# Block-causal attention and a gated convolution unit on one core: reciprocals spread by eight small transfers and a shuffle, attention output two pairs at a time, the first nine pairs interleaved anew

## Chip, cores and metric

The kernel runs on one core of a Trainium2 chip. The metric is the device time of the execution in microseconds (us). Before the change it is 261.77 us, the median of 13 runs (260.62 to 264.54).

## What is computed

Eight batches, eight heads, 576 positions of 64 features: attention in which a block of 64 positions sees itself and the blocks before it, and behind it a gated unit over the 512 joined features, with a causal convolution of five taps as the gate. Cut to what matters:

```python
scores = scale * np.matmul(q, k.transpose(0, 1, 3, 2))
scores = np.where(block_i >= block_j, scores, -1e9)
attn = np.exp(scores - np.max(scores, axis=-1, keepdims=True))
attn = attn / (np.sum(attn, axis=-1, keepdims=True) + 1e-09)
x = np.matmul(attn, v)                        # heads side by side: [8, 576, 512]
gate_pre = sum(conv_w[k] * xp[:, k:k + S, :] for k in range(5))
gate = 1.0 / (1.0 + np.exp(-gate_pre))
out = (gate * (x @ w_val)) @ w_out
```

All inputs and the output are fp32.

## The kernel before

The unit of work is a pair of heads of one batch: 32 pairs, t = 4b + n for pair n of batch b. The main loop (L398) takes one pair an iteration and runs on for LAG = 10 more, since the later stages of a pair follow in later iterations.

**Inputs.** `load_pair(hb)` loads q and k of half a batch (two pairs) as fp32 tiles `st` by four transfers on SyncE's queue (L99) and casts each to fp16 on GpSimd (L103), with VectorE and ScalarE in its place for the first half batch. Four buffers of `st` are there, so a load waits for the cast of two half batches before. The call for half batch t/2 + 3 stands in iteration t. `load_v` and `cast_v` (L106 to L124) do the same for v, once a batch, with one fp32 buffer and eight casts on GpSimd; the weights go through `st` too (L373 to L381). Matmuls and SyncE's transfers keep the order of the program (L43 to L47); on the other engines a scheduler chooses the order. Each transfer signals one of eight semaphores in turn, and waits until the transfer before it on the same semaphore has landed.

**Scores.** `trans` (L129) transposes a half batch in three parts of six 128 x 128 blocks on TensorE, and VectorE copies them out of PSUM into `qkT` (L143). `scores` (L157) makes a pair's scores transposed (keys on partitions) in four PSUM tiles, of which two buffers exist (`psS`), and ScalarE turns each into `pt` by an exp (L172, L197). No maximum is subtracted.

**Denominators.** `den` (L217) sums the columns of `pt` for the four pairs of a batch by matmuls with one-hot weights `oh`: row 32 * (2h + half) + n of the tile `dn` holds pair n's sums of head h and half block. VectorE takes the reciprocal `ri` (L250) of all 128 rows. `spread` (L253) brings them to the partitions that need them: `ri` to a DRAM scratch `r_scratch` (L255), and from there four broadcasts, each of four rows to 64 partitions, into `rb` (L260): 1.18 MB a batch.

**Attention output.** `pv` (L267) multiplies `pt` with v into two PSUM tiles `x` a pair, and VectorE multiplies them with `rb` into `xb` (L307), in fp16, features on partitions.

**Gated unit.** `gate` (L318) is the convolution as five matmuls with diagonal weights `diag` a half, and a tanh on ScalarE (L329); `val` (L332) multiplies `xb` of all four pairs by w_val, and VectorE joins both into `gv` (L346); `project` (L350) multiplies by w_out, 36 tiles in all, each copied on ScalarE (L357) and stored by its queue (L358). `conv_weights` (L361) makes `convT` and the 20 blocks of `diag` on VectorE (L369), in iterations 5 to 8.

All PSUM tiles but the scores' (`tr`, `dn`, `x`, `cv`, `vp`, `ot`) share one pool of four buffers, `psG` (L76).

The order within iteration t, by which TensorE's work is queued: scores of t (all of them at once while t < 10, later the first two tiles only), one output tile, `den` of the batch before where t is a multiple of 4, the loads, `spread` one iteration after `den`, `pv` of pair t - 6, the other two score tiles, `gate` of pair t - 10, a part of the transposes, `val` of pair t - 10, another part, another output tile.

Of the kernel before, what the change touches and what calls it, by code (L numbers as in the profile page):

```python
# [10 lines left out]
def kernel(  # L11
# [20 lines left out]
    nc = tc.nc  # L32
# [5 lines left out]

    B, H, S, D = q.shape
    NT = B * 4  # L40
    rscr = nc.dram_tensor("r_scratch", [B, 128, 288], fp32, kind="Internal")

    def mm(**kw):  # L43
        tc.keep_in_program_order(nc.tensor.matmul(**kw))  # L44

    def load(**kw):
# [11 lines left out]
    conv_nat = cpool.tile([5, 512], fp32, tag="conv_nat")  # L58
    convT = cpool.tile([128, 4, 5], fp32, tag="convT")
    diag = cpool.tile([128, 4, 5, 128], fp16, tag="diag")  # L60
    NXB = 3
    xbs = [cpool.tile([128, 4, S + 4], fp16, tag=f"xb{i}", name=f"xb{i}")
           for i in range(NXB)]
    vzs = [cpool.tile([128, 4, 6, 64], fp16, tag=f"vz{i}", name=f"vz{i}") for i in range(2)]

    stg = ctx.enter_context(tc.tile_pool(name="stg", bufs=4))
# [9 lines left out]
    psG = ctx.enter_context(tc.tile_pool(name="psG", bufs=4, space=PSUM))  # L76

    make_identity(nc, ident)
    nc.vector.tensor_copy(out=ident16[:, :], in_=ident[:, :])  # L79
    nc.vector.memset(oh[:, :, :], 0.0)  # L80
    for o, rows in enumerate((slice(0, 128), slice(0, 64), slice(64, 128))):
        nc.vector.memset(oh[rows, o, :].rearrange("p (m r) -> p m r", r=4)[:, :, 3:4], 1.0)
    for xb in xbs:
        nc.vector.memset(xb[:, :, 0:4], 0.0)
    for vz in vzs:
        nc.gpsimd.memset(vz[64:128, :, 0:5, :], 0.0)
        nc.gpsimd.memset(vz[0:64, :, 5, :], 0.0)
# [41 lines left out]
    def trans(hb, part):  # L129

        b, half = divmod(hb, 2)
        if b not in qkT:
            qkT[b] = qkp.tile([128, 4, 2, S], fp16, tag="qkT", name="qkT")
        tr = psG.tile([128, 6, 128], fp16, tag="G")
        slots = [divmod(6 * part + s, 9) for s in range(6)]
        for s, (w, c) in enumerate(slots):
            tc.keep_in_program_order(nc.tensor.transpose(  # L137
                out=tr[:, s, :], in_=q16[hb, w][:, c, :, :], identity=ident16[:, :]))
        for w in range(2):
            ss = [s for s in range(6) if slots[s][0] == w]  # L140
            if ss:
                c0 = slots[ss[0]][1]
                nc.vector.tensor_copy(  # L143
                    out=qkT[b][:, 2 * half:2 * half + 2, w, :].rearrange(
                        "p n (x c) -> p n x c", c=9)[:, :, :, c0:c0 + len(ss)],
                    in_=tr[:, ss[0]:ss[-1] + 1, :].rearrange("p c (x n) -> p n x c", n=2))
# [10 lines left out]
    def scores(t, part):  # L157
# [8 lines left out]
        def full(ps, h, i, lo):  # L166
            f = 64 * first_q(h, i)
            mm(out=ps[:, h, lo:lo + S - f], lhsT=kT[h][:, f - 64:f + 64], rhs=qT[h][:, f:S],
               start=True, stop=True, skip_group_check=True)
# [5 lines left out]
        if part == 0:  # L175
# [9 lines left out]
            full(ps, 1, 2, 320)  # L185
            ex(1024, ps[:, :, :], 1024)
            return
        ps = psS.tile([128, 2, 512], fp32, tag="S")
        full(ps, 0, 2, 0)
        q4 = [x.rearrange("d (j x) -> d j x", x=64) for x in qT]  # L190
        mm(out=ps[64:128, 1, 0:256], lhsT=kT[1][:, 0:64], rhs=q4[1][:, 1:8:2, :],
           start=True, stop=True, skip_group_check=True)
        for i in range(4):
            f = 64 * (2 * i + 1)
            mm(out=ps[0:64, 1, 64 * i:64 * i + 64], lhsT=kT[1][:, f:f + 64],
               rhs=qT[1][:, f:f + 64], start=True, stop=True, skip_group_check=True)
        nc.scalar.activation(  # L197
            out=pt[:, 2048:2560].rearrange("p (h x) -> p h x", h=2),
            in_=ps[:, :, 0:256], func=AF.Exp, bias=0.0, scale=0.125)
        ps = psS.tile([128, 2, 512], fp32, tag="S")  # L200
        mm(out=ps[64:128, 0, 0:320], lhsT=kT[1][:, 0:64], rhs=q4[1][:, 0:9:2, :],
           start=True, stop=True, skip_group_check=True)
# [9 lines left out]


    ris = {}
    rbs = {}

    def den(b):  # L217

# [33 lines left out]

    def spread(b):  # L253

        load(out=rscr[b], in_=ris.pop(b)[:, :])  # L255
        rb = rp.tile([128, 4, 2, 288], fp32, tag="rb")
        for h in range(2):
            for e in range(2):
                r0 = 32 * (2 * h + e)
                load(  # L260
                    out=rb[64 * h:64 * h + 64, :, e, :],
                    in_=rscr[b, r0:r0 + 4, :].rearrange("(a r) x -> a r x", a=1).to_broadcast(
                        [64, 4, 288]))
        rbs[b] = rb


    def pv(t):  # L267
        b, n = divmod(t, 4)
        pt = pts.pop(t)
        v16, vd, vz = vts[b]  # L270
        xb = xbs[b % NXB]
        for part, (lo, hi) in enumerate(((0, 5), (5, 9))):
            nb = hi - lo
            x = psG.tile([128, nb, 64], fp32, tag="G")
# [27 lines left out]
            for z in range(max(len(x_) for x_ in todo)):  # L302
# [4 lines left out]
            nc.vector.tensor_tensor(  # L307
                out=xb[:, n, 4 + 64 * lo:4 + 64 * hi].rearrange("p (j e y) -> p j e y", e=2, y=32),
                in0=x[:, :, :].rearrange("p j (e y) -> p j e y", e=2),
                in1=rbs[b][:, n, :, :].rearrange("p e (j y) -> p j e y", y=32)[:, lo:hi],  # L310
                op=ALU.mult)


# [45 lines left out]
                          in_=ob[:, :])  # L359

    def conv_weights(g):  # L361
        if g == 0:
            ps = psG.tile([128, 4, 16], fp32, tag="G")
            for i in range(4):
                mm(out=ps[:, i, 0:5], lhsT=conv_nat[0:5, 128 * i:128 * i + 128],
                   rhs=ident[0:5, 0:5], start=True, stop=True, skip_group_check=True)
            nc.vector.tensor_copy(out=convT[:, :, :], in_=ps[:, :, 0:5])
        for j in range(5):
            nc.vector.tensor_scalar(out=diag[:, g, j, :], in0=ident16[:, :],  # L369
                                    scalar1=convT[:, g, j:j + 1], scalar2=0.0,  # L370
                                    op0=ALU.mult, op1=ALU.add)
# [22 lines left out]
    load_pair(2)  # L394

    proj = []
    LAG = 10
    for t in range(NT + LAG):  # L398
        b, r = divmod(t, 4)
        m = t - LAG  # L400
        hb = (t + 3) // 2 if t % 2 else t // 2 + 1
        tr = [(hb, part) for part in ((1, 2), (0,))[t % 2]] if hb < 2 * B else []
        if t < NT:
            scores(t, 0)
            if m < 0:
                scores(t, 1)
        if t == 0:
            trans(1, 0)
        if proj:
            project(*proj.pop(0))  # L410
        if r == 0 and 1 <= b <= B:
            den(b - 1)
        if t % 2 == 0:
            load_pair(t // 2 + 3)
        if r == 0 and b < B:
            load_v(b)
        if t in (2, 3, 6, 7):
            weights(t // 4, t % 2 * 2)
        if r == (2 if b else 1) and b < B:
            cast_v(b)  # L420
        if r == 1 and 1 <= b <= B:
            spread(b - 1)
        if 0 <= t - 6 < NT:
            pv(t - 6)
        if 0 <= m and t < NT:
            scores(t, 1)
        if 5 <= t < 9:
            conv_weights(t - 5)
        if 0 <= m < NT:
            gate(*divmod(m, 4))  # L430
        if tr:
            trans(*tr.pop(0))
        if 0 <= m < NT:
            val(*divmod(m, 4))
            u, i = divmod(m, 8)
            if i == 3:
                proj.extend((u, j) for j in range(4))
            if i == 7:
                proj.extend((u, j) for j in range(4, 9))
        if tr:  # L440
            trans(*tr.pop(0))
        if proj:
            project(*proj.pop(0))
# [32 lines left out]
```

## Time and profile before

The times are those of one profiled execution on the slowest core (here the only one).

| | |
|---|---|
| profiled execution | 261.69 us |
| its span, first to last instruction | 259.9 us |
| TensorE matmul (PE) | 222.1 us busy, 85% |
| TensorE weight load (PEld) | 154.1 us, 59% |
| VectorE (DVE) | 124.7 us, 48% |
| ScalarE (ACT) | 136.4 us, 52% |
| GpSimd (POOL) | 91.5 us, 35% |
| moved by DMA | 50.94 MB, 196 GB/s |
| chain that ended last: `rb<-r_scratch` and `r_scratch<-ri` | 8% and 7% of the span |

A row of the profile names the source line, the engine, the operation, the output and the input, then the busy time and mean time of one. "issue" stands for time in which an engine waited for nothing that the profile shows; SPq is the queue of SyncE, which only issues transfers. A busy TensorE need not be at its peak: ends of matmuls are modelled. The shares are averages over stages that differ much, so that the tables by stage are to be read first.

### The profile page before, as it was taken

What the parts mean: (1) busy time and instruction counts of PE and PEld (TensorE: products, weight loads), DVE (VectorE), ACT (ScalarE), POOL (GpSimd) and SP (SyncE); (2) the same over time, 40 slices, a digit from 0 to 9 for tenths busy, and PEclk for the clock granted to TensorE, in tenths of its full rate; (3) what the DMA queues carried; (4) which work ended last, traced back from release to release, by engine and by line L of the source; (5) the groups of instructions that cost most, each with busy time, mean ns of one, the idle gap of its engine ahead of it and who ended that gap; (6) DMA issues with size and microseconds to landing.
All of it is one profiled execution on the core that took longest, in us unless ns stands there. A gap on an engine that the chain in (4) does not pass through costs nothing.

```text
span 259.9 us, 7172 instructions
## 1 busy us (share of the span) xinstructions
PE 222.1 (85%) x3064; PEld 154.1 (59%) x3064; DVE 124.7 (48%) x230; ACT 136.4 (52%) x230; POOL 91.5 (35%) x108
## 2 busy tenths in 40 slices
PE   0387787658788898988999999999999999999993
PEld 0255375437556665666667766776676667667661
DVE  2532447954544653474446545663456326254130
ACT  0357637412744465655665666556655661332533
POOL 5444952826283382315730564063005300000000
PEclk9999996757799999999999999999999999999999
DMA  6999586898789959887995699666816421921305
GB/s 193 310 291 261 200 237 152 170 344 249 157 177 366 211 116 304 296 203 156 339 282 157 160 322 281 179 149 156 226 55 159 117 83 34 238 98 43 139 27 202
DMA packets 34730, 50.94 MB, mean 196 GB/s; under 512 B 2437, under 2 KB 20869, under 8 KB 34698
## 3 DMA queue, kind: packets, MB, share of 16 engines
q1 hardware_dynamic: 29504, 41.03, 59.7%
q10 hardware_dynamic: 5194, 9.45, 9.7%
q8 instruction: 24, 0.39, 0.7%
q14 instruction: 8, 0.07, 0.1%
HBM read 39.86 MB, written 10.62 MB: 194 GB/s over the span
## 4 chain that ended last, share of the span: by engine, by line
PE 62%; DMA 18%; ACT 9%; DVE 6%; SPq 3%; issue 2%; DVEq 0%; ACTq 0%
PE cv L44 14%; PE ot L44 11%; PE vp L44 10%; PE ps L44 9%; DMA rb<-r_scratch 8%; ACT pt L172 8%; DMA r_scratch<-ri 7%; PE x L44 6%; PE dn L44 6%; PE tr L137 6%; SPq L47 3%; DVE qkT L143 3%; DVE ri L250 2%; DMA st<-in_k_dram 2%; DMA out_dram<-ob 1%
## 5 line engine op out<-in xcount | busy, mean ns | idle before, releaser
L172 ACT ACTIVATE pt<-ps 128x1024 f16<-128x1024 f32 (+1 forms) x96 | 76.1, 828 | 47.8 <-PE ps L44 47.5
L143 DVE COPY qkT<-tr 128x768 f16<-128x768 f16 (+1 forms) x64 | 50.1, 830 | 45.1 <-PE tr L137 45.0
L44 PE MATMUL ps<-qkT 64*64 64x64 f16 (+10 forms) x608 | 49.7, 269 | 14.4 <-ACT pt L172 12.5
L103 POOL CAST t<-st 128x1152 f16<-128x1152 f32 x30 | 34.3, 1145 | 44.6 <-DMA st<-in_q_dram 24.8
L44 PEld LDWEIGHTS <-qkT 64*64 64x64 f16 (+1 forms) x608 | 24.3, 110 | 38.3 <-issue 30.3
L44 PE MATMUL cv<-xb,diag 128*128 128x288 f16 x320 | 45.5, 286 | 1.6 <-DVE xb L307 1.1
L357 ACT COPY ob<-ot 128x512 f32<-128x512 f32 x36 | 21.3, 591 | 36.4 <-PE ot L44 34.9
L346 DVE SCALAR_TENSOR_TENSOR gv<-th,vp 128x288 f16<-128x288 f32 x64 | 27.2, 447 | 27.5 <-PE vp L44 27.0
L307 DVE TENSOR_TENSOR xb<-x,rb 128x320 f16<-128x320 f32 x64 | 26.2, 445 | 29.3 <-PE x L44 19.9
L116 POOL CAST t<-st 128x2304 f16<-128x2304 f32 x8 | 16.9, 2106 | 65.6 <-PE x L44 53.3
L137 PE MATMUL tr<-ident,t 128*128 128x128 f16 x288 | 28.2, 250 | 13.7 <-DVE ident L79 6.9
L44 PE MATMUL vp<-xb,w_val_sb 128*128 128x288 f16 x256 | 37.0, 286 | 2.0 <-issue 1.3
L329 ACT ACTIVATE th<-cv 128x288 f32<-128x288 f32 x64 | 26.2, 410 | 23.0 <-PE cv L44 22.8
L44 PE MATMUL ot<-w_out_sb,gv 128*128 128x512 f16 x144 | 35.8, 380 | 0.3
L44 PEld LDWEIGHTS <-diag 128*128 128x128 f16 x320 | 28.9, 97 | 11.7 <-issue 2.0
L137 PEld LDWEIGHTS <-t 128*128 128x128 f16 x288 | 22.8, 112 | 16.5 <-DVE t L103 6.8
L44 PE MATMUL x<-pt,t 128*64 128x256 f16 (+3 forms) x384 | 28.4, 261 | 1.6 <-DVE qkT L143 1.5
L44 PEld LDWEIGHTS <-w_val_sb 128*128 128x128 f16 x256 | 24.1, 98 | 8.3 <-issue 2.0
L44 PEld LDWEIGHTS <-t 128*64 128x64 f16 x384 | 18.9, 114 | 10.1 <-issue 7.6
L250 DVE RECIPROCAL ri<-dn 128x288 f32<-128x288 f32 x8 | 15.7, 1957 | 19.2 <-PE dn L44 19.2
L197 ACT ACTIVATE pt<-ps 128x512 f16<-128x512 f32 x32 | 19.2, 599 | 5.5 <-PE ps L44 5.5
L44 PEld LDWEIGHTS <-gv 128*128 128x128 f16 x144 | 12.9, 98 | 15.0 <-issue 2.3
(31 smaller groups left out, 138.2 us busy)
## 6 DMA issues: line engine op xcount, KB each, us to landing
st<-in_q_dram SPq DMA_DIRECT2D x32, 288.0 KB, 6.3
st<-in_k_dram SPq DMA_DIRECT2D x32, 288.0 KB, 6.0
rb<-r_scratch SPq DMA_DIRECT2D x32, 288.0 KB, 5.5
out_dram<-ob ACTq DMA_DIRECT2D x36, 256.0 KB, 2.7
r_scratch<-ri SPq DMA_DIRECT2D x8, 144.0 KB, 2.6
st<-in_moe_w_val_dram SPq DMA_DIRECT2D x2, 512.0 KB, 7.2
st<-in_moe_w_out_dram SPq DMA_DIRECT2D x2, 512.0 KB, 8.1
st<-in_v_dram SPq DMA_DIRECT2D x8, 0.2 KB, 9.8
```

Of the source, the lines that this page charges most:

```text
L44: tc.keep_in_program_order(nc.tensor.matmul(**kw))
L103: cast(out=t[:, :, :, :], in_=st[:, :, :, :].rearrange("p z c d -> p c z d"))
L116: nc.gpsimd.tensor_copy(out=t[:, :, :], in_=st[:, :, :])
L137: tc.keep_in_program_order(nc.tensor.transpose(out=tr[:, s, :], in_=q16[hb, w][:, c, :, :], identity=ident16[:, :]))
L143: nc.vector.tensor_copy(out=qkT[b][:, 2 * half:2 * half + 2, w, :].rearrange("p n (x c) -> p n x c", c=9)[:, :, :, c0:c0 + len(ss)], in_=t ...
L172: nc.scalar.activation(out=pt[:, o:o + w], in_=src, func=AF.Exp, bias=0.0, scale=0.125)
L197: nc.scalar.activation(out=pt[:, 2048:2560].rearrange("p (h x) -> p h x", h=2), in_=ps[:, :, 0:256], func=AF.Exp, bias=0.0, scale=0.125)
L250: nc.vector.reciprocal(out=ri[:, :], in_=dn[:, :, :].rearrange("p j x -> p (j x)"))
L307: nc.vector.tensor_tensor(out=xb[:, n, 4 + 64 * lo:4 + 64 * hi].rearrange("p (j e y) -> p j e y", e=2, y=32), in0=x[:, :, :].rearrange("p ...
L329: nc.scalar.activation(out=th[:, HF * hf:HF * hf + HF], in_=cv[:, :], func=AF.Tanh, bias=0.0, scale=0.5)
L346: nc.vector.scalar_tensor_tensor(out=gvs[u][:, g, c0:c0 + HF], in0=th[:, HF * hf:HF * hf + HF], scalar=1.0, in1=vp[:, :], op0=ALU.add, op1 ...
L357: nc.scalar.copy(out=ob[:, :], in_=ot[:, :])
```

## The change

Five things change together.

- `spread` no longer goes through DRAM. Eight transfers of 4 rows x 288 values (4.6 KB) take `ri` from SBUF to a tile `rq` (two of them, filled with 1.0 at the start) so that in each quadrant of 32 partitions the rows 0 to 3 hold the four pairs' reciprocals of both half blocks of that head. For batch 0 the four transfers of the first head go by ScalarE's queue.
- `pv` begins with a shuffle on VectorE, which copies row n of each quadrant of `rq` to all its 32 rows, 576 fp32 elements, into a `rb` for this pair alone.
- `pv` runs for two pairs in the iterations t = 4b + 3 (pairs 0 and 1 of batch b - 1) and t = 4b + 4 (pairs 2 and 3), and in the other two not at all; the third and fourth score tile stand between the two. LAG is 9.
- While t < 9, `scores` goes in three parts (two tiles, one, one), with parts of the transposes between them. `conv_weights` moves to iterations 0 to 4.
- At the start ScalarE runs a dummy exp of one column, and copies the second part of the first half batch's transposes in VectorE's place.

In the changed program VectorE meets the first shuffle of a batch two iterations after the reciprocal for batches 0 and 1 and at the end of the reciprocal's own iteration from batch 2 on. For batch 0 ScalarE's four issues stand within and behind the exps of iteration 5.

The diff, cut to its core:

```diff
-    rscr = nc.dram_tensor("r_scratch", [B, 128, 288], fp32, kind="Internal")
...
+    rqs = [cpool.tile([128, 2, 288], fp32, tag=f"rq{i}", name=f"rq{i}") for i in range(2)]
...
+    nc.vector.memset(coefs[:, :], 0.0)
+    nc.scalar.activation(out=coefs[:, :], in_=coefs[:, :], func=AF.Exp, bias=0.0, scale=1.0)
...
+    for rq in rqs:
+        nc.gpsimd.memset(rq[:, :, :], 1.0)
...
-                nc.vector.tensor_copy(
+                evac = nc.scalar.copy if hb == 0 and part == 1 else nc.vector.tensor_copy
+                evac(
...
-        load(out=rscr[b], in_=ris.pop(b)[:, :])
-        rb = rp.tile([128, 4, 2, 288], fp32, tag="rb")
+        ri = ris.pop(b)
         for h in range(2):
-            for e in range(2):
-                r0 = 32 * (2 * h + e)
-                load(
-                    out=rb[64 * h:64 * h + 64, :, e, :],
-                    in_=rscr[b, r0:r0 + 4, :].rearrange("(a r) x -> a r x", a=1).to_broadcast(
-                        [64, 4, 288]))
-        rbs[b] = rb
+            for u in range(2):
+                for e in range(2):
+                    r0, r1 = 32 * (2 * h + u), 32 * (2 * h + e)
+                    move = nc.scalar.dma_start if b == 0 and h == 0 else load
+                    move(out=rqs[b % 2][r0:r0 + 4, e, :], in_=ri[r1:r1 + 4, :])
...
+        rb = rp.tile([128, 2, 9, 32], fp32, tag="rb")
+        nc.vector.stream_shuffle(out=rb[:, :, :, :].rearrange("p e j y -> p (e j y)"),
+                                 in_=rqs[b % 2][:, :, :].rearrange("p e x -> p (e x)"),
+                                 mask=[n] * 32)
...
-                in1=rbs[b][:, n, :, :].rearrange("p e (j y) -> p j e y", y=32)[:, lo:hi],
+                in1=rb[:, :, lo:hi, :].rearrange("p e j y -> p j e y"),
...
-    LAG = 10
+    LAG = 9
...
+        if t == 0:
+            tr.insert(0, (1, 0))
         if t < NT:
             scores(t, 0)
-            if m < 0:
-                scores(t, 1)
-        if t == 0:
-            trans(1, 0)
-        if proj:
-            project(*proj.pop(0))
-        if r == 0 and 1 <= b <= B:
-            den(b - 1)
...
+        if t <= 4:
+            conv_weights(t - 1)
+        if proj:
+            project(*proj.pop(0))
+        if r == 0 and 1 <= b <= B:
+            den(b - 1)
+        if m < 0 and tr:
+            trans(*tr.pop(0))
+        for n in range(2):
+            if r == 3 and 1 <= b <= B:
+                pv(4 * b - 4 + n)
+            if r == 0 and 2 <= b <= B + 1:
+                pv(4 * b - 6 + n)
+            if n == 0 and t < NT:
+                if 0 <= m:
+                    scores(t, 1)
+                    scores(t, 2)
+                else:
+                    scores(t, 1)
+                    if tr:
+                        trans(*tr.pop(0))
+        if m < 0 and t < NT:
+            scores(t, 2)
         if r == 1 and 1 <= b <= B:
             spread(b - 1)
-        if 0 <= t - 6 < NT:
-            pv(t - 6)
-        if 0 <= m and t < NT:
-            scores(t, 1)
-        if 5 <= t < 9:
-            conv_weights(t - 5)
```

## The prediction

> **What bounds the kernel now.** I read the windows by stage first, the chain second, then the time lines of the queues. Let t be the loop's pair number; the four denominators of t = 4, 8, 12, 16 begin at 33.3, 59.6, 83.4 and 110.9 us in TensorE's time line, which gives the stretches below (microseconds, busy time of PE, PEld, DVE, ACT, POOL with instruction counts, granted clock, DMA share, GB/s).
>
> ```profile
> 13.07:32.90 19.83, 15.35 (x133) 9.35 (x133) 6.97 (x9) 13.58 (x19) 12.17 (x14) 1.00 0.84 245
> 32.90:59.60 26.70, 19.05 (x260) 14.28 (x259) 17.17 (x34) 11.79 (x17) 13.28 (x16) 0.72 0.84 225
> 59.60:82.90 23.30, 18.87 (x314) 14.13 (x313) 11.90 (x20) 10.59 (x18) 11.54 (x14) 0.88 0.87 233
> ...
> 138.20:163.50 25.30, 24.74 (x382) 17.23 (x382) 13.36 (x24) 16.68 (x29) 10.75 (x12) 1.00 0.80 226
> ```
>
> A full stage (138 to 163) is TensorE work from end to end. The first three do a third to two thirds of such a stage's work in as much time. Why, the chain tells (start, length, what):
>
> ```profile
> 38.21 6.96 DMA r_scratch<-ri
> ...
> 47.18 7.97 DMA rb<-r_scratch
> ...
> 55.23 0.50 DVE xb L307
> ...
> 64.27 6.80 DMA r_scratch<-ri
> ...
> 73.06 6.52 DMA rb<-r_scratch
> ...
> 79.66 0.50 DVE xb L307
> ```
>
> From 38 to 55 and from 64 to 80 us nothing but the reciprocals' way to DRAM and back ends the waits. Behind it SP's queue stands still, so the next loads leave late; and they are late already, as SyncE's and GpSimd's time lines show:
>
> ```profile
> 24.44 2.11 POOL L116 CAST t<-st 128x2304 f16<-128x2304 f32 x1 [3.74 <-DMA st<-in_v_dram]
> 30.80 2.23 POOL L103 CAST t<-st 128x1152 f16<-128x1152 f32 x2
> ...
> 31.97 1.20 SPq L47 DMA_DIRECT2D st<-in_q_dram  x2
> 33.27 1.19 SPq L47 DMA_DIRECT2D st<-in_k_dram  x2
> 34.92 0.71 SPq L47 DMA_DIRECT2D st<-in_v_dram  x1
> 38.21 4.22 SPq L47 DMA_DIRECT2D r_scratch<-ri  x1
> 45.19 2.61 SPq L47 DMA_DIRECT2D rb<-r_scratch  x4
> 47.89 2.11 SPq L47 DMA_DIRECT2D st<-in_q_dram  x2
> ```
>
> The values of batch 0 land at 24.4, GpSimd casts them until 30.7, and only then the fifth half batch of q and k (needed at t = 5), whose staging buffers the sixth waits for. The load of v sent at 34.9 lands at 44.9, and r_scratch, queued behind it, at 45.2.
>
> **TensorE's work at the full clock**, start to start in the time line around 104 to 112 us: scores 1.12 a pair, six transposes 0.34 (16 half batches x 3), attention output 0.84, conv 1.24, value product 0.98, one output tile 0.97, denominators 1.54 a batch. From t = 10 on (68.8 us) there remain 22 scores 24.6, 29 transposes 9.9, 6 denominators 9.2, 28 outputs 23.5, 32 conv 39.7, 32 value 31.4, 36 tiles 34.9: 173.2. With 4.0 from the last matmul to the end, the 191.1 us to 259.9 hold 13.9 of loss. So the kernel's time is the start of t = 10, plus 173.2, plus 4.0, plus losses, and the change is to be costed in these terms.
>
> **Head.** The table load (1.28 us at 7.88, right before k's cast) moves ahead, behind the wait for k: gain 1.3. Two of the four PSUM copies go from DVE to ACT, which then runs two of about 0.5 (estimate from ACT's 436 ns for 320 and 599 for 512 elements) beside DVE's 0.96: together scores start at about 11.3, not 13.1. The GpSimd fills of rq (two of 576 elements; 1.16 us was measured for 1280) lie in its idle 5.1 us before the first cast: nothing.
>
> **t = 0 to 4.** Now scores, exps and transposes take turns: ACT has 2.98 a pair (1.94 + 0.60 + 0.44) and pairs start at 18.2, 22.0, 26.4, 30.2: about 4.1 apart. With transposes put between score parts the pitch falls to the larger of ACT's 2.98 and TensorE's. Here a row and a rule differ: the clock row says full speed until 40 us, but the same seven score matmuls take 1.03 there and 0.61 at 90 us. TensorE: Matmul & The Clock Gate (Part 1, The HAM clock gate) says that the array starts at half clock until it has been busy for a window of some 3.4 us, and warns that the recorded clock is not to be trusted alone. By the row TensorE needs 1.12 + 0.51 = 1.6 a pair; by the durations 2.0 + 1.05 = 3.05. I take 3.2, and the den of t = 4 in between: t = 5 starts at 30. The 20 diag instructions (7.8 us of DVE), moved from t = 5..8 to t = 1..4, make DVE 17.9 us busy from 11.3 on, until 29.2: just covered; in the kernel now they hold a transposed tile back by 1.3 us at 52.
>
> **t = 5 to 9.** The loads rule: the casts for t = 5, 6 end at about 31.4 and 32.5 as now (0.5 earlier), those for t = 7, 8 at 36.7 and 40.6. The spread leaves 8 transfers of 4.6 KB instead of 147 KB out and four broadcasts of 288 KB back (9.4 MB of the 50.9 in all). For batch 0 four go out on ACT's queue: 4 x 0.56 of issue there, and the last waits until w_val has landed (34), at worst 1.4 us of exps behind it. The other four stand in SP's queue behind v of batch 1, as r_scratch does now, and land with it at 45.3. The next q, k loads leave at 40.6 instead of 47.9. Two pairs of attention output at t = 7 take all four PSUM buffers; they come free when VectorE has shuffled (two of 0.75) and multiplied: 47.2. den of t = 8 waits for that, about 5 us. Then VectorE's order is counted through: reciprocal until 52.0, copies 53.3, products 54.2, copy 55.1, products 56.0; TensorE starts t = 9 at 54.3, conv and value product included now, and t = 10 at **58.1** instead of 68.8.
>
> **The shuffle** has no row. Below: the slope of the product (474 ns for 320, 416 for 256 elements: 0.91 ns an element) gives 0.71 for 576; above: the reciprocal's 1.96 for 288 elements would give 3.7. VectorE: DVE Perf Modes (the perf-mode tier table) has it at one element a cycle, some 2400 ns for 2048, which with the same fixed part is 0.77. I take 0.75, near the product's row since both read one element at a time: 32 x 0.75 = 24 us, VectorE 124.7 to 149 of 250. A stage has 13.4 to 15.2 us of VectorE in 25 to 28; 3 more stay under it. From 3.7 us a shuffle it would be the bound.
>
> **A rule against the change.** DMA: Bandwidth & Descriptors (Rules for kernel authors) says to coalesce small transfers; under 64 KB one pays mostly overhead (its Anatomy of one DMA puts the fixed part at some 2 us). Eight in a row, waited for one by one, would be 16 us. The rows: a DMA issue takes SP 0.61 us, r_scratch lands after 1.8 to 2.6 from 110 us on, 5.7 to 7.0 before. So 8 x 0.61 + 1.8 = 6.7 after the reciprocal, against 1.8 + 2.6 + 5.5 = 9.9 now. I take 6.7 for late batches, 10 to 12 for the first.
>
> **Full stages.** SP's other loads stand behind 4.9 us of issues instead of about 4.4 of waiting and issuing: even. From batch 2 on, VectorE's first shuffle waits at the end of t = 4b + 4 for the spread, with copies and gate products queued behind it. Counted through, VectorE reaches it 5.3 us after the reciprocal, and TensorE can go on for 4.9 more before it lacks a buffer; less the 2.4 of shuffles and copy behind it, a landing up to 7.8 us after the reciprocal costs nothing. What does cost: in two of four iterations no attention output lies between scores any more. TensorE has 0.55 + 0.97 + 0.28 us before the third score tile, whose buffer the second exp frees at 2.45: 0.65 lost, twice a batch: 1.3 x 5 batches = 6.5. Given back: the two waits for rb at 79 and 101 us (1.1 + 1.0) and the half-clock stretch at t = 10 (1.2 to 1.4). Losses 13.9 - 2.1 - 1.4 + 6.5 = 16.9. Conv and value product of one pair (2.2) are done by t = 10, so 171.0 remain.
>
> **Sum:** 58.1 + 171.0 + 4.0 + 16.9 = 250.0 of span; the profiled run has 1.8 outside its span (261.69 and 259.9) and lies 0.1 under the median: about 251.5.
>
> **Rivals.** (1) As summed, own range 246 to 257: half the chance. (2) The early waits are shorter: SP's half of the first spread isn't held by v's load, so that products come at 41 and t = 10 at 53, and the third tile's wait is partly covered (losses 12): 53 + 171 + 4 + 12 + 1.8 = 242. For it: four transfers on ACT's own queue; against: r_scratch landed 0.3 us after v. 0.25. (3) The early gain is mostly hidden: TensorE falls back to half clock in the 5 us wait, den, outputs and copies each late, t = 10 at 64: 258. The clock row's 0.50 at 55 to 60 us speaks for it. 0.12. (4) Slower: the shuffle at the head of VectorE's queue. If the eight transfers land as r_scratch does early (7.0) in every batch, 4.9 + 7.0 = 11.9 is 4.1 over the 7.8, in 6 batches: 25 us, 276. It decides from 9.5 us after the reciprocal (1.7 a batch eats the gain of 10.3). Against it: 1.8 us landings from 140 us on. 0.13.
>
> **Numbers.** 251.5; range 241 to 261, which takes in (2) and (3) and leaves out (4) and a little under (2). Within 0.2%, what a measurement can hardly tell from no change, 0.03; faster 0.84; slower 0.13.
>
> **What would show it.** Score start near 11.3; pairs 3.2 apart until t = 4; first product near 47; t = 10 near 58; DMA about 42 MB; shuffles of 0.75; per full stage two waits of TensorE for exp of 0.65; products never waiting for a spread after 110 us. Wrong if shuffles take over 1.5, if spreads land more than 9 us after a reciprocal in full stages, or if t = 10 starts after 66.

## The result, and the profile after

The changed kernel takes 256.45 us, the median of 11 runs (254.24 to 258.59); the kernel before, run beside it, 262.37 us (48 runs). The ratio is 0.9775, with a 95% interval of 0.9747 to 0.9803: 2.2% faster. The prediction was 251.5 us in a range of 241 to 261. The profiled execution of the changed kernel took 258.59 us (span 256.8), the slowest of its eleven and 2.1 us above the median, so that its early stages have to be held against other runs, as is done below.

First the windows by stage, as before: TensorE's time line has the denominators of t = 4, 8, 12 at 28.6, 47.0 and 75.5 us (33.3, 59.6 and 83.4 before). The columns are the stretch, its length, the busy time of PE, PEld, DVE, ACT and POOL with counts, granted clock, DMA share, GB/s.

```profile
11.90:28.59 16.69, 15.56 (x134) 9.72 (x135) 13.75 (x30) 11.83 (x17) 9.63 (x11) 0.84 0.90 258
28.59:47.00 18.41, 14.07 (x249) 10.10 (x248) 10.25 (x16) 13.04 (x18) 9.82 (x10) 0.87 0.72 204
47.00:75.52 28.52, 24.70 (x347) 18.18 (x347) 17.84 (x37) 11.96 (x21) 19.62 (x24) 0.82 0.75 218
131.43:158.72 27.29, 25.47 (x384) 17.73 (x382) 17.10 (x34) 16.29 (x29) 10.75 (x12) 1.00 0.55 172
```

From the first scores to the denominators of t = 4, and from there to those of t = 8, it takes 16.7 and 18.4 us instead of 20.2 and 26.3. In the third row, 347 matmuls need 24.70 us of TensorE at a granted clock of 0.82. The last row is a full stage: 27.29 us long where the like one before had 25.30, with TensorE busy 25.47 of it instead of 24.74 of 25.30. So the start won and the full stages lost.

The chain (start, length, what) at the place where before r_scratch and rb had stood:

```profile
35.22 7.76 DMA rq<-ri
...
43.00 1.74 DMA rq<-ri
...
45.06 0.86 DVE rb L278 x2
...
46.45 0.50 DVE xb L316
...
47.00 2.90 PE dn L43 x72
```

One way of the reciprocals in place of two: it ends at 44.7 instead of 55.2. SyncE's and GpSimd's time lines for the same stretch:

```profile
24.09 2.11 POOL L121 CAST t<-st 128x2304 f16<-128x2304 f32 x1 [4.09 <-DMA st<-in_v_dram]
30.48 2.23 POOL L108 CAST t<-st 128x1152 f16<-128x1152 f32 x2
...
34.79 0.71 SPq L46 DMA_DIRECT2D st<-in_v_dram  x1
37.35 6.23 SPq L46 DMA_DIRECT2D rq<-ri  x4
43.68 1.27 SPq L46 DMA_DIRECT2D st<-in_q_dram  x2
```

The values still land at 24.1 and hold GpSimd until 30.5. Four small transfers behind v's next load keep SyncE's queue for 6.23 us (3.16 of them the first issue alone, the one directly behind that load), and the loads of q and k leave at 43.7 (47.9 before). The shuffle's row of the page (busy time, mean ns of one), and that of the loads' queue (packets, MB, share):

```profile
L278 DVE STREAM_SHUFFLE rb<-rq 128x576 f32<-128x576 f32 x32 | 24.8, 806 | 0.1
...
q1 hardware_dynamic: 20128, 30.69, 41.0%
```

In the page before, that queue had moved 41.03 MB, and the whole 50.94 instead of 40.62.

The account in stages, by the starts of the denominators in the time line: t = 12 comes 7.9 us earlier (75.5 for 83.4). From t = 12 to t = 32 the five stages take **137.2 us instead of 130.1**:

```profile
83.38:213.46 130.08, 124.22 (x1880) 85.64 (x1877) 66.97 (x120) 81.79 (x142) 47.46 (x55) 1.00 0.74 201
75.52:212.68 137.16, 127.63 (x1881) 87.64 (x1878) 82.54 (x161) 82.29 (x142) 46.90 (x54) 1.00 0.46 142
```

The first row is the kernel before, the second the changed one; both run at a granted clock of 1.00. From t = 32 to the end it is 44.1 instead of 46.4. That is work moved and not work saved: with the lag of 9 the 18 matmuls of one pair's convolution and value product stand ahead of t = 12 instead of behind t = 32 (445 matmuls there for 463). Together -7.9 + 7.1 - 2.3 = -3.1, the difference of the spans (256.8 and 259.9). The question is therefore which part of the change wins the start, and which one loses the full stages.

### The profile page after: what moved, and what is told of

Same layout as the page of the kernel before. It is cut to its first block, busy times and chain, and to the rows that moved or that the text cites. A ratio compares the mean times of both kernels' runs of the same rounds, so it can differ in the third digit from the quotient of the medians.

```text
span 256.8 us, 7299 instructions
## 1 busy us (share of the span) xinstructions
PE 223.1 (87%) x3064; PEld 154.5 (60%) x3064; DVE 146.1 (57%) x293; ACT 138.3 (54%) x233; POOL 92.3 (36%) x110
## 2 busy tenths in 40 slices
DMA packets 25386, 40.62 MB, mean 158 GB/s; under 512 B 2053, under 2 KB 11525, under 8 KB 25354
## 4 chain that ended last, share of the span: by engine, by line
PE 50%; ACT 13%; DMA 12%; DVE 8%; issue 6%; SPq 5%; POOL 4%; ACTq 0%; DVEq 0%; POOLq 0%
PE cv L43 16%; ACT pt L178 11%; PE vp L43 9%; PE ot L43 7%; PE x L43 6%; DMA rq<-ri 6%; PE ps L43 5%; SPq L46 5%; PE dn L43 5%; DMA st<-in_v_dram 4%; DVE qkT L149 3%; DVE ri L257 3%; PE tr L142 3%; DMA st<-in_k_dram 2%; ACT ob L366 1%
## 5 line engine op out<-in xcount | busy, mean ns | idle before, releaser
L149 DVE COPY qkT<-tr 128x768 f16<-128x768 f16 (+1 forms) x62 | 49.2, 834 | 47.3 <-PE tr L142 47.3
L43 PEld LDWEIGHTS <-qkT 64*64 64x64 f16 (+1 forms) x608 | 24.9, 104 | 43.8 <-issue 36.6
L43 PE MATMUL cv<-xb,diag 128*128 128x288 f16 x320 | 47.0, 295 | 0.2 <-DVE gv L355 0.2
L43 PEld LDWEIGHTS <-diag 128*128 128x128 f16 x320 | 29.8, 100 | 10.3 <-issue 0.5
L43 PE MATMUL x<-pt,t 128*64 128x256 f16 (+3 forms) x384 | 27.4, 255 | 2.7 <-DVE ri L257 2.0
L142 PEld LDWEIGHTS <-t 128*128 128x128 f16 x288 | 21.9, 109 | 12.6 <-DVE t L108 6.8
L316 DVE TENSOR_TENSOR xb<-x,rb 128x320 f16<-128x320 f32 x64 | 25.5, 445 | 3.9 <-PE x L43 3.8
L278 DVE STREAM_SHUFFLE rb<-rq 128x576 f32<-128x576 f32 x32 | 24.8, 806 | 0.1
```

What stands on the lines that cost most here:

```text
L142: tc.keep_in_program_order(nc.tensor.transpose(out=tr[:, s, :], in_=q16[hb, w][:, c, :, :], identity=ident16[:, :]))
L149: evac(out=qkT[b][:, 2 * half:2 * half + 2, w, :].rearrange("p n (x c) -> p n x c", c=9)[:, :, :, c0:c0 + len(ss)], in_=tr[:, ss[0]:ss[-1] ...
L278: nc.vector.stream_shuffle(out=rb[:, :, :, :].rearrange("p e j y -> p (e j y)"), in_=rqs[b % 2][:, :, :].rearrange("p e x -> p (e x)"), ma ...
L316: nc.vector.tensor_tensor(out=xb[:, n, 4 + 64 * lo:4 + 64 * hi].rearrange("p (j e y) -> p j e y", e=2, y=32), in0=x[:, :, :].rearrange("p ...
```

## The experiments

Three theories on the full stages. A: the third and fourth score tiles, which follow the second at once, wait for the exps. B: the shuffles, 3.2 us of VectorE a stage, stand in front of what frees TensorE's PSUM buffers. C: the attention output two pairs at a time is the cause, since two of four iterations have no products to cover exps and the other two have double. "Step" below is an iteration t; the five stages from t = 12 to t = 32 are called the full stages. Each kernel's ratio is to the kernel before, run beside it.

**1. The fourth score tile later.** Edit to the changed kernel:

```diff
                 if 0 <= m:
                     scores(t, 1)
-                    scores(t, 2)
...
+        if 0 <= m and t < NT:
+            scores(t, 2)
         if 0 <= m < NT:
             gate(*divmod(m, 4))
```

> The changed kernel, with the fourth score tile of a pair put behind the gate in the full stages (t of 9 and more), nothing else. Theory A (the full stages lose what the start gains, because TensorE waits for the exp that frees the tile's buffer, some 0.6 to 0.8 us in three of four iterations): stages from t = 12 to 32 fall from 137 to about 129 us, the time by 6 to 8, ratio to the kernel before about 0.95; no wait of TensorE for exp over 0.3 us is left there. Theory B (the full stages lose to VectorE, which the shuffles load and hold up): stages as they are, time within 1.5 us of the changed kernel, ratio about 0.975.

Measured: 258.99 us, ratio 0.9885 [0.9834, 0.9936]; full stages 140.2. What TensorE waited for in them (total us, times, longest), first in the changed kernel, then in this one:

```profile
PE ps L43 <- ACT pt L178: 6.6, 17, 0.4
PE x L43 <- DVE ri L257: 1.1, 4, 0.3
```

```profile
PE vp L43 <- DVE qkT L149: 6.0, 8, 0.9
PE x L43 <- DVE ri L257: 1.9, 5, 0.4
PE ps L43 <- ACT pt L178: 0.4, 2, 0.2
```

The waits for exps are gone (6.6 to 0.4), as A wanted, but the value product now waits 6.0 us for a PSUM buffer that VectorE empties by the copy into `qkT`. The wait has changed its place, and the stages are 3.0 us longer. Neither theory's ratio came (0.95 and 0.975). A names the right place, but not the cure: putting one tile elsewhere doesn't fill steps that have too little work.

**2. New order, old spread.** The changed kernel with `r_scratch`, the four broadcasts and `rb` of the kernel before, no shuffle:

```diff
-        ri = ris.pop(b)
+        load(out=rscr[b], in_=ris.pop(b)[:, :])
...
-                in1=rb[:, :, lo:hi, :].rearrange("p e j y -> p j e y"),
+                in1=rbs[b][:, n, :, :].rearrange("p e (j y) -> p j e y", y=32)[:, lo:hi],
```

> The changed kernel's order with the old way of the reciprocals through DRAM and no shuffle (the start, the two pairs at a time and LAG 9 stay). Theory A (the spread itself gains at the first two batches, the order of the full stages loses): the first products come at 52 to 55 us instead of 46.5, t = 10 starts 6 to 9 us later, the full stages lose as much as now; ratio 1.00 to 1.01. Theory B (shuffles load the full stages): full stages back to 130 us, ratio 0.97 to 0.98. If the new start alone makes the gain, ratio 0.975.

Measured: 268.57 us, ratio 1.024 [1.0174, 1.0305]: slower than before the change. Its full stages take 138.7 us, with no shuffle anywhere. Theory A had 1.00 to 1.01: the start is ahead of the kernel before at t = 8 (54.0 for 59.6 us), but has lost that by t = 12 (83.9 for 83.4).

**3. Old order, new spread.** The kernel before with the eight transfers, `rq` and the shuffle only, so that LAG, the order of the steps and the head stay:

```diff
-        load(out=rscr[b], in_=ris.pop(b)[:, :])
+        ri = ris.pop(b)
...
+                    move = nc.scalar.dma_start if b == 0 and h == 0 else load
+                    move(out=rqs[b % 2][r0:r0 + 4, e, :], in_=ri[r1:r1 + 4, :])
...
+        nc.vector.stream_shuffle(out=rb[:, :, :, :].rearrange("p e j y -> p (e j y)"),
```

> The kernel before with the new spread (small transfers and a shuffle a pair) and nothing else: order, LAG 10 and start as before. Theory A: the 14 us that the chain spends at 38 to 55 us and the 15 at 64 to 80 us shrink to the landing of v (about 45 and 71), full stages stay near 130: time 252 to 257, ratio 0.96 to 0.98. Theory B (shuffles cost in the full stages): gain at the start lost again, ratio 0.99 to 1.01. If pairs one at a time meet the shuffle sooner than the spread lands, products wait in every batch: over 1.01.

Measured: 258.82 us, ratio 0.988 [0.9813, 0.9947]; full stages 130.6 with all 32 shuffles. The total lies between what A and B had forecast; the stages decide. B falls: 2 and 3 show that the new order makes the full stages long (138.7 without a shuffle) and that the shuffles don't (130.6 in the old order). The spread by itself is worth 3 us in the old order; in the new one it is worth 12 (268.57 to 256.45).

**4. The values' load behind the spread.** In the changed kernel the load of the next batch's v moves from ahead of `spread` in SyncE's queue to behind it:

```diff
-        if r == 0 and b < B:
+        if t == 0:
             load_v(b)
...
         if r == 1 and 1 <= b <= B:
             spread(b - 1)
+            if b < B:
+                load_v(b)
```

> The changed kernel with the load of v of a batch issued behind the spread of the batch before instead of ahead of it. Theory A (the first spread lands at 45 us because its four transfers on SP's queue stand behind v's 4608 short rows): the first shuffle starts at 40 to 42 us instead of 45, TensorE's wait before the denominators of t = 8 goes, the time falls by 2 to 4 us: ratio 0.962 to 0.97. Rival: the spread waits for k of the same half batch anyway (its semaphore), lands at 42 to 43, and v comes 5 to 7 us later to GpSimd, which holds up the casts of q and k behind it: no gain or 1 to 4 us slower than the changed kernel, ratio 0.975 to 0.99.

Measured: 255.10 us, ratio 0.9737 [0.966, 0.9814], an interval that still holds the changed kernel's 0.9775; the theory's 0.962 to 0.97 did not come. In its time line the first shuffle starts at 40.7 us instead of 45.1; the denominators of t = 8 begin at 46.2 instead of 47.0. Four microseconds at the shuffle are worth less than one at the next stage: the early spread was not the only thing that step 8 waited for. Nor do the next loads gain: the first load of q, now directly behind v's, takes 4.73 us to issue, so that the loads of k behind it leave at 45.3, as in the changed kernel (45.1). The hold-up behind v has moved on to the next transfer.

**5. Pairs apart, lag 9.** On top of 4, from batch 1 on the first two pairs of batch b - 1 come one each in the steps 4b + 2 and 4b + 3, and only the last two together:

```diff
-            if r == 3 and 1 <= b <= B:
-                pv(4 * b - 4 + n)
+            if r == 3 and b == 1:
+                pv(n)
+            if n == 0 and r in (2, 3) and 2 <= b <= B:
+                pv(4 * b - 6 + r)
```

> As e5 (values of a batch loaded behind the spread), and from batch 1 on the first two pairs of a batch are multiplied one each in the steps 4b+2 and 4b+3 instead of both in 4b+3; the last two stay together in 4b+4, the first batch and the gate lag of 9 stay as after the change. Theory C (the full stages lengthen because two steps in four hold no products, so that TensorE runs ahead of the exps there, and two hold double): half of the unevenness goes, the four stages and the last to the start of den at step 32 take 133 to 135 us (137.1 with e5), the waits for exps about 3 us instead of 6.6, total 251 to 253. Rival D (the third and fourth score tiles directly behind the second are to blame, whatever the products do): the stages stay at 136.5 to 138, total 255.

**6. Pairs apart, lag 10.** On top of 4, only the first batch in twos; then one pair in each step, and the gate as late as before the change:

```diff
-    LAG = 9
+    LAG = 10
...
-            if r == 3 and 1 <= b <= B:
-                pv(4 * b - 4 + n)
-            if r == 0 and 2 <= b <= B + 1:
-                pv(4 * b - 6 + n)
+            if r == 3 and b == 1:
+                pv(n)
+            if t == 8:
+                pv(2 + n)
+            if n == 0 and 10 <= t < NT + 6:
+                pv(t - 6)
```

> As e5 at the start (first batch's pairs two at a time in steps 7 and 8), then one pair in each step from step 10 on and the gate 10 steps behind, which is the order of the kernel before in its full stages except for where the projection and den stand. Theory C: the stages from den at step 12 to den at step 32 take 130 to 131.5 us as they do before the change, total about 250 to 252 (6 us of stages won, up to 2 lost because the gate starts one unit later). Rival D: 135 or more, total above 254. If the lag of 9 was itself what the gain at the start rests on, the start of den at step 12 stays but the end comes 2 us or more later than the stages say.

Measured: 5 takes 252.54 us, ratio 0.9656 [0.9593, 0.9718], full stages 133.2. 6 takes **249.03 us, ratio 0.9539 [0.9477, 0.9602]**, full stages 130.2. The waits of TensorE in 6's full stages:

```profile
PE ot L43 <- DVE gv L355: 3.0, 4, 1.0
PE ps L43 <- ACT pt L178: 2.0, 5, 0.4
```

The more evenly the products lie, the shorter the stages: 137.1 (kernel 4), 133.2, 130.2. The waits for exps fall with them: 6.6 us (kernel 4), 4.5, 2.0. This is what C said. Kernel 6 changes the lag as well, though; experiment 9 parts the two. Kernel 6 beats both the kernel before and the changed one.

**7. Pairs apart from the first.** The changed kernel with one pair a step throughout and LAG = 10:

```diff
-            if r == 3 and 1 <= b <= B:
-                pv(4 * b - 4 + n)
-            if r == 0 and 2 <= b <= B + 1:
-                pv(4 * b - 6 + n)
+            if n == 0 and 0 <= t - 6 < NT:
+                pv(t - 6)
```

> As after the change, but with one pair in each step six steps behind from the first pair on and the gate lag of 10, both as before the change; the new head, loads, casts and the new spread stay. The first product is then due in step 6, some 7 us before the first spread has landed (45 us). Theory: TensorE stands still in step 6 for about 9 to 11 us instead of 5 in step 8, den of batch 1 moves from 47.0 to 51 to 54, and the full stages fall to 130 to 132; the two cancel, total 254 to 258. Rival (the two-at-a-time order gives nothing at the start): den of batch 1 stays at 47 to 48 and the total is 249 to 251.

Measured: 251.23 us, ratio 0.9602 [0.9542, 0.9661]; full stages 130.0. The denominators of t = 8, though:

```profile
46.96 2.60 PE L43 MATMUL dn<-pt,oh 128*32 128x160 f16 x88 [3.04 <-DVE xb L316]
```

They begin when they did with the pairs in twos (47.0). My expectation of 51 to 54 missed and the rival was right: at the start the twos gain nothing that can be seen here.

**8. The same with the values' load behind the spread** (4's edit on top of 7), which leaves the first batch's order as the only difference from 6:

> As e8 (one pair in each step from the first on, gate 10 steps behind) with the load of the values of a batch behind the spread, as in e5 and e12. It differs from e12 only in the first batch, whose pairs come apart in steps 6 to 9 instead of in twos in steps 7 and 8. Theory (pairs in twos buy nothing even there, since VectorE's wait for the spread ends at the same time): 248.5 to 250.5, den of batch 1 at 46 to 48. Rival (twos shield the scores of steps 6 and 7 from the first spread): den of batch 1 at 49 to 51, total 251 to 253.

Measured: 250.21 us, ratio 0.9561 [0.9492, 0.963], denominators of t = 8 at 45.8, full stages 129.8. The interval covers 6's: twos or not in the first batch can't be told apart.

**9. The gate one step earlier, pairs apart.** Kernel 6 with LAG = 9 for 10.

> As e12 (one pair a step from step 10 on) with the gate 9 steps behind instead of 10, so that a gate unit runs in the step of its batch's last pair. Theory C (the two-at-a-time order is the cost, the lag is not): full stages from den at step 12 to den at step 32 stay at 130 to 131.5 us, TensorE finds a unit more at step 9, the total is 248 to 250. Rival (a lag of 9 needs pairs in twos: with one pair a step the gated product waits in every fourth step for VectorE's multiplication): 0.5 to 1 us in each of the seven such steps, 252 to 256.

Measured: 252.27 us, ratio 0.9635 [0.9578, 0.9692]; full stages 132.5, at a granted clock of 1.00. The rival was right. TensorE's waits in its full stages:

```profile
PE cv L43 <- DVE xb L316: 4.2, 5, 1.0
PE ps L43 <- ACT pt L178: 2.5, 7, 0.4
```

With one pair a step the last pair of a batch is multiplied in the very step whose convolution reads it, and VectorE isn't done. The kernel also parts twos and lag. It has the lag of kernel 4 and the pairs of kernel 6: of the 6.9 us between the full stages of these two (137.1 and 130.2), 4.6 go with the twos and 2.3 with the lag of 9. The waits for exps go with the twos alone: 6.6 us in kernel 4, 2.5 here, 2.0 in kernel 6. So C holds for the larger part. What the lag of 9 saves behind t = 32 (44.4 us instead of 46.4) is again one pair's work that stands ahead of t = 12 instead.

**10. A second shuffle.** The changed kernel with one more shuffle of the same size a pair, into a buffer `rx` that nobody reads:

```diff
+        rx = rp.tile([128, 2, 9, 32], fp32, tag="rx")
+        nc.vector.stream_shuffle(out=rx[:, :, :, :].rearrange("p e j y -> p (e j y)"),
```

> As after the change with one more shuffle of the same size per pair into a buffer that nobody reads: 32 more of 0.80 us on VectorE, 25.6 us more in all. Theory (VectorE is not what bounds a full stage: 17.3 us of about 28.5 are busy): 3.2 us more per stage hide, the total is 0 to 2 us above the changed kernel (256.5 to 258.5). Rival (the shuffles stand in front of reads that free TensorE's banks, and so lengthen the stages): 5 us or more per batch of double pairs, up to 0.8 us for each of 16 double steps, 262 to 270.

Measured: 264.47 us, 8.0 more than the changed kernel (5.7 by the profiled spans); ratio 1.0059 [1.0013, 1.0105]. By the total the rival had it. By the stages it had not: the last four before t = 32 take 28.6, 27.3, 28.6 and 25.4 us, to the tenth those of the changed kernel, with VectorE busy 166.9 us instead of 146.1. The loss lies ahead of them, where VectorE was already the late one: at t = 8 the second shuffles put the reciprocal at 51 and TensorE waits 2.7 us for a PSUM buffer, and the next stage (32.0 instead of 27.4) has a hole that the waits give as

```profile
PE ps L43 <- issue: 3.4, 1, 3.4
```

"issue" means that the profile shows nothing it waited for. Holes of this kind, of 0.3 to 1.6 us, stand in other kernels as well; what made this one stays open, and whether it is in every execution too.

**11. The head undone.** No dummy exp, all copies of the first transposes on VectorE:

```diff
-    nc.scalar.activation(out=coefs[:, :], in_=coefs[:, :], func=AF.Exp, bias=0.0, scale=1.0)
...
-                evac = nc.scalar.copy if hb == 0 and part == 1 else nc.vector.tensor_copy
+                evac = nc.vector.tensor_copy
```

> As after the change, but the head is undone: no exp ahead of the loads and all copies of the first transposes on VectorE. By the prediction's first step the scores then start 1.8 us later (13.7 instead of 11.9 us) and, if nothing downstream absorbs it, the whole is 1.8 us longer: 257.5 to 258.5. Rival (the loads of steps 5 to 8 set when the first products run, so that 1.8 us at the start are absorbed by the wait for the first spread): the scores start later all the same, den of batch 1 stays within 0.7 us of 47.0, total 256 to 257.

Measured: 258.16 us, ratio 0.9891 [0.9808, 0.9974]. The scores start at 13.1 instead of 11.9, 1.2 us later and not 1.8; the denominators of t = 8 at 49.1 instead of 47.0. The head's gain is passed on whole: 2.1 at t = 8, 1.7 in the medians.

**12. The first spread wholly on ScalarE's queue.** Kernel 6 with

```diff
-                    move = nc.scalar.dma_start if b == 0 and h == 0 else load
+                    move = nc.scalar.dma_start if b == 0 else load
```

> As e12 with all eight transfers of the first spread issued from ScalarE's queue. In e12 the four on SyncE's queue leave between 34.2 and 39.6 us and hold the next loads of q and k until 41.0; without them these leave at 35 to 36. Cost: four more issues of about 0.58 to 0.7 us stand in front of the exps on ScalarE (2.5 us). Theory (the loads are what the steps behind 47 us wait for): den of step 12 comes 1 to 3 us earlier than 70.5, total 246.5 to 248.5. Rival (exps are): den at 47.2 moves to 48.5 to 49.5, total 249.5 to 251.

Measured: 252.54 us, ratio 0.9659 [0.9609, 0.9709]: 3.5 us slower than kernel 6, more than the rival gave it. ScalarE's time line:

```profile
34.87 7.94 ACTq L269 DMA_DIRECT2D rq<-ri  x7
42.85 1.94 ACT L178 ACTIVATE pt<-ps 128x1024 f16<-128x1024 f32 x2 [7.56 <-DMA rq<-ri]
```

The issues themselves took what I had put on them, 0.58 us in the median and 1.44 at most. But the first row is a stretch and not a sum: six were out by 39.43, the seventh left at 42.22 only. Together they held the exps back by 7.56, and what ended the wait is, by the profile, the landing of one of them. That fits the rule that a transfer waits for the one before it on its semaphore; the profile doesn't name the semaphore. The denominators of t = 8 slide to 52.2. SyncE's loads didn't leave early either, at 42.9.

## Why the prediction was right, and where its sizes were off

The mechanism was the one forecast: the way of the reciprocals through DRAM had set t = 5 to t = 9, its removal pulls the start ahead, and the full stages give a part back. The time, 256.45 us, lies within the range and 5.0 above the number. Against the profiled span (256.8 instead of 250.0) the difference of 6.8 us splits into two terms: t = 10 starts at 61.3 and not at 58.1 (+3.2), and from there it takes 195.5 us and not 191.9 (+3.6). Of the second, 1.3 to 1.6 lie between t = 10 and t = 12, at a lower clock than in kernels 4 and 11 (14.2 us against 12.6 and 12.9), and 1.6 in the full stages. The sum itself makes 251.9, not 251.5: 250.0 of span, 1.8 outside it and 0.1 to the median.

- **Head.** Forecast 11.3, measured 11.9. Right; experiment 11 shows its gain passed on to t = 8.
- **t = 0 to 4.** Forecast 3.2 us a pair: in ScalarE's time line the first exps of t = 1 and t = 4 start at 18.66 and 28.27, 3.2 apart each. The first pair takes 6.1 instead: the small matmuls that turn the convolution's weights (1.86 us at 12.87, not in my sum) come between. So t = 5 starts at about 32.5 and not at 30, which the wait for the first spread takes up. VectorE is busy without a gap from 20 to 28.9: the 20 `diag` blocks are just covered, as forecast. This stretch is also the place of the weighing between clock row and durations. The durations were the right choice: the seven matmuls at 18.0 us still take 1.03 us while the clock row reads 1.00 from 18 to 20. The pitch can't confirm it, since 3.2 lies near ScalarE's 2.98 as well as near TensorE's 3.05. The warning of the Trainium skill's page TensorE: Matmul & The Clock Gate (Part 1, The HAM clock gate) that the recorded clock is not to be trusted alone agrees with this. Its window of some 3.4 us can't be seen in this trace: at 18.0 TensorE had been busy without a wait for 6.1.
- **Loads and the first spread.** The casts and v's load are where they were put. The first shuffle comes at 45.1 (landing forecast 45.3), the denominators of t = 8 at 47.0 (forecast 47.2). The next loads leave at 43.7 and not at 40.6, since the four issues took 6.23 us from end to end and not 2.4: the first took 3.16, and before the fourth the queue stood for 1.2. The "first product" mark was put wrongly: the matmuls of the first products run from 41.1 into free PSUM buffers, and only their multiplication waits, so that TensorE stands 1.5 us ahead of the denominators and not 5.
- **t = 8 and 9: the step that was too small.** From the denominators of t = 8 to the scores of t = 10 the sum had 10.9 us; measured were 14.3. Rival 3's mechanism, a fall of the clock, was a part of it, though behind a wait of 1.5 us and not of 5. The same stretch in three kernels, first the changed one, then kernels 4 and 11 (whose order in it is the same):

```profile
47.00:61.33 14.33, 12.43 (x201) 9.52 (x200) 9.07 (x17) 4.60 (x8) 11.16 (x14) 0.76 0.86 256
```

```profile
46.19:58.86 12.67, 9.45 (x203) 7.14 (x202) 7.05 (x11) 6.11 (x10) 10.69 (x13) 1.00 0.79 267
```

```profile
49.08:61.16 12.08, 9.22 (x201) 7.12 (x200) 8.56 (x16) 5.81 (x10) 8.18 (x9) 1.00 0.90 285
```

The same 201 to 203 matmuls need 12.4 us of TensorE at a clock of 0.76 and 9.2 to 9.5 at 1.00; the convolution of t = 9 takes 2.39 us in the first and 1.40 in the others. So some 1.7 to 2.3 of the 3.4 us go with the clock in this one execution (an estimate, since kernels 4 and 11 differ from it ahead of this stretch), and 1.2 to 1.8 were counted too tightly by me. The clock also accounts for much of what this execution lies above the median: with it the stage from t = 8 to t = 12 takes 28.5 us, in kernels 4 and 11 25.2 and 25.0. The runs of the changed kernel alone spread by 4.3 us.
- **The shuffle.** Forecast 0.75, measured 0.81; the prediction's other estimate, 0.77 from the figure of the Trainium skill's page VectorE: DVE Perf Modes (the perf-mode tier table), came a little nearer. Its cost in full stages is about zero, by experiment 3 and by the last stages of experiment 10. Near the front, where VectorE is late anyway, it isn't free (experiment 10).
- **The rule against the change.** The Trainium skill's page DMA: Bandwidth & Descriptors (Rules for kernel authors) speaks for few large transfers. Where the queue is free, eight small ones took 6.4 to 6.6 us from the reciprocal's end to the first shuffle (79.1 to 85.5, 106.5 to 113.1; forecast 6.7), far from eight fixed parts in a row (the page gives its 2 us for transfers that GpSimd issues; these are SyncE's). Early it was 12.2 (32.8 to 45.0; forecast 10 to 12). The slower rival had wanted early landings in every batch; they didn't come. VectorE does wait for spreads, 11.1 us in all, but TensorE holds out, as the 7.8 us of cover said. Small transfers have their price in the queues, though: SyncE's was held for 6.23 us by four, ScalarE's for 7.94 by seven.
- **Full stages: the forecast term came, others were missing.** The sum had +6.5 for score tiles that wait for exps in steps without products. Of the 3.5 given back only the wait for rb at 101 us (1.0) lies in the full stages; it did go. The half clock at t = 10 did not in this execution (the convolution there takes 2.58 us). So the forecast for t = 12 to t = 32 was +5.5, and +7.1 was measured. The forecast loss can be seen line by line, first in the kernel before, then in the changed one at t = 21, a step without products:

```profile
99.00 0.64 PE L44 MATMUL ps<-qkT 64*128 64x256 f16 x12
```

```profile
141.43 0.51 PE L43 MATMUL ps<-qkT 64*128 64x256 f16 x6
142.35 0.34 PE L43 MATMUL ps<-qkT 64*64 64x320 f16 x6 [0.41 <-ACT pt L178]
```

The third and fourth tile of a pair run on in one go where two pieces of other work (an output tile and products, or denominators and products) stand ahead of them; where only one does, the fourth waits. From start to end 0.64 us become 1.26, so a break costs 0.62, of which the profile shows 0.41 as a wait and the rest as longer busy time. The kernel before has one such break a stage, the changed one three: ten more in five stages, 6.2 us, and two shorter waits of 0.23. The prediction had 0.65, twice a batch, and called the tile the third. In the full stages of the kernel before, the waits for exps are

```profile
PE ps L44 <- ACT pt L172: 2.0, 5, 0.4
```

and after the change 6.6 us. They show only part of the loss: the score matmuls' busy time rises too, from 25.5 to 27.9 us for the same 376, and is 25.5 again in kernel 6. What the sum did not have are 1.1 us of waits for a PSUM buffer behind the reciprocal and some 2 us that no line names. That the number still came near has some luck in it: two holes of the kernel before, 2.2 us at 89 and 117 us that its profile calls issue, shrink to 0.2 in the profile after. I had it as a wait of one tile; experiment 1 shows that it is the step as a whole that lacks work, and experiments 5, 6 and 9 that laying the products evenly takes most of it back.

What each part is worth, then, by the ratios and some 262 us before: the new spread alone wins 3.1 us (experiment 3), the new order with the new head alone loses 6.3 (2), both together win 5.9, and 10.4 with the pairs apart and the lag of 10 (7). The two-at-a-time order with its lag was thus the part that cost, about 4.5 us, and by experiment 9 mostly the order. With v's load moved as well the kernel wins 12.1 (6), though 4, 6, 7 and 8 by themselves don't resolve what the load adds.

## What to carry to other kernels

When a loop's step on the busiest engine is a mixture that covers another engine's latency, moving one ingredient out of half of the steps can cost even if the sum of work stays the same (here 4.6 us in five stages): count the work of each step, not of the stage. Read a change with several parts by stage before judging it, since a gain at the start and a loss in the steady state can belong to different parts, and the second can be taken out. A transfer through DRAM that the steady state hides can still set a start-up stage by its two landings, and small transfers between partitions shorten it only as far as the queue that they stand in lets them.

## What the runs showed of the hardware

- What stands directly behind a load of v is held. In the fourteen traces of this case every issue on SyncE's queue that takes longer than 1.6 us (1.8 to 7.1) is the one right behind a load of v, whether it moves q, `r_scratch` or a small transfer. Not each one there is so long; why it happens stays open. Otherwise a small transfer's issue takes 0.58 us in the median, and eight in a row keep the queue for 5.07.
- Transfers issued by ScalarE hold its own work: with seven of them (0.58 us each in the median) between its exps, the next exp came 7.56 us late.
- A shuffle of 128 x 576 fp32 elements within quadrants takes 0.79 to 0.85 us on VectorE, about 1.4 ns an element, and its mask load 10 to 30 ns.
- The same order ran one early stage at a granted clock of 0.76 in the changed kernel's profiled execution and at 1.00 in those of kernels 4 and 11: 201 matmuls took 12.43 us of TensorE, or 9.22. So a time mark in such a start is good to some 2 us only.
